# Two more slots, a smaller DMA scratch and one wide last group of y in a fused attention and feed-forward kernel

## The chip, the cores and the metric

The kernel runs on one core of one Trainium2 chip. The metric is the device time of one execution in microseconds (us), smaller is better; a single profiled execution supplies the trace. TensorE is called PE in the rows, VectorE DVE, ScalarE ACT, GpSimd POOL, SyncE SP.

## What is computed

Attention with rotary positions over 2 batches, 8 heads, 576 positions and 64 values per head, then two feed-forward blocks on the 1152 x 512 result x:

```python
a = x @ w_a                  # 512 -> 1536
b = x @ w_b
x = (a * b) @ w_out          # the first block; its result is called y in the kernel
h = x @ w_in                 # 512 -> 2048
g = h - np.tanh(h)
out = g @ w_out2             # the second block
```

The weights of both blocks arrive as 64-bit floats, seen by the kernel as pairs of 32-bit integers.

## The kernel before

**Precision.** Every matmul of the feed-forward blocks is done in three: each operand is split into a high part (a copy that rounds) and a low part (what is left), and high x high, high x low and low x high are added in PSUM (`mm3`, L517; the o matmuls do the same at L1204).

**Weights.** A list `units` (L407) fixes the order in which weights are brought in: for the first block ("ab", f) for each of its 12 chunks of 128, with ("o", f // 2) for each pair; for the second block ("i", n) and ("2", n), n = 0 to 7, in the order i0, i1, 2_0, 2_1, i2, i3, 2_2, 2_3 and so on. ("i", n) holds w_in for chunks 2n and 2n + 1, ("2", n) holds w_out2 for the same two chunks. Each unit is one DMA (two for "ab") on SyncE's queue into one of two staging tiles `st` (L428), and then a conversion in four pieces (`conv_unit`, L448): ScalarE scales one word and VectorE shifts the other (L457, L458); VectorE combines them in two passes (L460, L464), and after the second ScalarE casts the high part into its final place (L481); VectorE subtracts for the low part (L483). The staging tile is free for the next DMA when L483 is done. `cv(n)` emits n pieces and is called between the matmul groups; `get_w` (L500) emits whatever is missing where a matmul asks for it.

The final place of an "ab" or "i" weight is one of two halves of a tile `w0`, if one is free at that moment in the order of the code. Otherwise, and always for "o" and "2", it is a tile of the common pool `slots`, of which weights may hold `wcap` at a time: 6 (WC1) in the first block, 4 (WC2) in the second. `retire` (L505) gives the place back in that order once the last matmuls that read the weight are emitted.

**The common pool.** `slots` (L1045) has 12 tiles of 9 KB per partition. They hold `tmpa` for the whole rest of the kernel, the weights just named, the products `g` of the chunks (high and low part of a * b in the first block, of h - tanh(h) in the second), and in the second block `tmpb` and, for its chunks 0 and 1 only, `hs`. A tile that finds no free slot waits until one is released.

**First block.** For each chunk f, `ab_unit` (L1059) does 3 x 24 matmuls for a and b (three stretches of 384 tokens), ScalarE copies a out of PSUM (L1064), VectorE multiplies by b (L1065), ScalarE casts the high part of g (L1068) and VectorE subtracts for the low part (L1069). After every second chunk, 12 y units are queued, one for each of 3 stretches of tokens and 4 stretches of 128 outputs; six are emitted after each of the next chunks. A y unit (`y_unit`, L1075) is 6 matmuls, over the two chunks of its group, into one PSUM bank, and then a sum into `yacc`: a ScalarE copy for the first group (L1086), a VectorE addition for the other five (L1088). In the last group each unit also splits its sum for the second block: ScalarE casts `yh` (L1096), and the subtraction for `yl` (L1097) is on VectorE for odd d and on GpSimd for even d. The last group's units use only the four PSUM banks of one side, since the four of the other side go to the second block.

**Second block.** For each of its 16 chunks, `h_unit` (L1142) does 36 matmuls into one of two PSUM tiles of three banks, taken in turn. Then follows a chain between ScalarE and VectorE: squares (L1164, L1167), a mask written into g's tile (L1168), a polynomial (L1169, L1174), tanh (L1173), h - tanh (L1177), the choice between the two (L1178), the high part (L1179) and the low part (L1180). L1168 is the first write into a new g, so it is what waits for a slot. Chunk f + 2 can use chunk f's PSUM tile when L1177 is done; chunks 0 and 1 are first copied to `hs` (L1159), so that tanh is the last reader. After every four chunks, 9 o units (`o_unit`, L1188) are queued, each 12 matmuls of 512 columns over the group's four chunks for 128 tokens, and three are emitted after each of the next chunks. The sum into `oacc` is a ScalarE copy for the first group (L1210) and a VectorE addition later (L1212); the o units of all groups but the last share two PSUM banks. The last group's results leave by DMA.

**Order.** Up to the end of the attention a list written by hand orders all engines. From there on the framework's scheduler orders each engine's instructions: what is emitted first goes first among what is ready by the scheduler's own estimate, so a matmul group can be started in parts. On the chip each engine then works in that fixed order.

Of the kernel before, what the change touches and what calls it, by code (L numbers as in the profile page):

```python
CFG = {'WC1': 6, 'WC2': 4, 'CY': 1, 'CA': 2, 'CH': 2, 'OE': 3, 'PA': 99, 'PB': 0, 'PO': 4, 'GA': 0, 'GB': 0, 'WF': 99, 'WCE': 5, 'NH': 2, 'HA': 0, 'NT2': 2, 'NW': 20, 'TM': 1, 'CO': 1, 'CHB': 0, 'WG': 99, 'WCG': 4, 'XL': 7}
# [1 line left out]

# [13 lines left out]
ALU = mybir.AluOpType  # L17
# [341 lines left out]
def attention_moe_kernel(  # L359
# [13 lines left out]
    nc = tc.nc  # L373
# [4 lines left out]
    P = 128  # L378
    NPAIR = H // 2
    KC = DM // P  # L380
    NF1 = FF1 // P
# [4 lines left out]
    NP3 = 3  # L386
    TP = NT // NP3
    NTT = NT // P
    CW = 9
    globals().update(CFG)  # L390

    def hp(k):
        o = CFG.get('P_' + k, 0)
        return tc.high_priority(offset=o) if o else nullcontext()
# [100 lines left out]
    def cv(n):  # L495
        for _ in range(n):
            if not next(pieces, False):
                break

    def get_w(key):  # L500
        while key not in conv:
            assert next(pieces)
        return conv[key][0]

    def retire(key):  # L505
        hold = conv.pop(key)[1]
        if hold is None:
            nslot[0] -= 1
        else:
            wfree.append(hold)  # L510
# [6 lines left out]
    def mm3(ps, w, x, start, stop):  # L517
        for n, (a, c) in enumerate(((0, 0), (0, 1), (1, 0))):
            nc.tensor.matmul(ps, w(a), x(c), start=start and n == 0, stop=stop and n == 2)  # L519
# [3 lines left out]
    def m_tile(name, side=None):  # L523
        nps[0] += 1
        return psm[nps[0] % len(psm) if side is None else side].tile([P, 512], F32, tag="m", name=name)[:, 0:TP]
# [3 lines left out]
    def ab_mm(f, t):  # L529
        if (f, t) in ab_ps:  # L530
            return
        wc = get_w(("ab", f)).rearrange("p s (m c f) -> p s m c f", m=2, c=KC)
        r = []
        for m in range(2):
            ps = m_tile("ab")
            for c in range(KC):
                mm3(
                    ps, lambda s: wc[:, s, m, c],
                    lambda s: xt[s][:, c, t * TP:(t + 1) * TP], c == 0, c == KC - 1,
                )  # L540
            r.append(ps)
        ab_ps[f, t] = r


    with ExitStack() as actx:
# [48 lines left out]
        ps = {}  # L594
# [33 lines left out]
        def half(j):  # L628
            return slice(64 * j, 64 * j + 64)
# [385 lines left out]
        for i in range(2):  # L1015
            nc.vector.tensor_copy(
                out=qb[half(i), :, half(1 - i)], in_=zero[half(i)].rearrange("p (s x) -> p s x", s=2)
# [24 lines left out]
                conv["ab", f] = (cbuf["w0"][:, f], f)  # L1042


    slots = ctx.enter_context(tc.tile_pool(name="slots", bufs=12))  # L1045
    cbuf["slots"] = slots
    wcap[0] = WC1
    tmpa = slots.tile([P, 2, NP3, TP], F32, tag="slot", name="tmpa")
# [4 lines left out]
    with m2ctx:  # L1053
        psm.append(m2ctx.enter_context(
            tc.tile_pool(name="ps_m2", bufs=4, space=bass.MemoryType.PSUM, side="left")
        ))
        pf = {}

        def ab_unit(f):  # L1059
            a = tmpa[:, f % 2]  # L1060
            for t in range(NP3):
                ab_mm(f, t)
                r = ab_ps.pop((f, t))
                nc.scalar.copy(out=a[:, t], in_=r[0])  # L1064
                nc.vector.tensor_tensor(out=a[:, t], in0=a[:, t], in1=r[1], op=ALU.mult)  # L1065
                cv(1)
            g = slots.tile([P, 2, NP3, TP], F32R, tag="slot", name="g")
            nc.scalar.copy(out=g[:, 0], in_=a)  # L1068
            (nc.gpsimd if GA <= f < GB else nc.vector).tensor_tensor(out=g[:, 1], in0=a, in1=g[:, 0], op=ALU.subtract)  # L1069
            pf[f] = g  # L1070
            retire(("ab", f))

        GY = 2

        def y_unit(g, t, d):  # L1075
            last = g == NF1 // GY - 1
            ps = m_tile("y", 1 if last else None)
            for c in range(GY):
                wc = get_w(("o", (g * GY + c) // 2)).rearrange("p s (c d) -> p s c d", c=2)
                mm3(  # L1080
                    ps, lambda s: wc[:, s, c % 2, d * P:(d + 1) * P],
                    lambda s: pf[g * GY + c][:, s, t], c == 0, c == GY - 1,
                )
            o = yacc[:, d, t * TP:(t + 1) * TP]
            if g == 0:
                nc.scalar.copy(out=o, in_=ps)  # L1086
            else:
                nc.vector.tensor_tensor(out=o, in0=o, in1=ps, op=ALU.add)  # L1088
            if (t, d) == (NP3 - 1, KC - 1):
                for c in range(0, GY, 2):  # L1090
                    retire(("o", (g * GY + c) // 2))
            if last:
                if not yt:
                    yt.extend(actp.tile([P, KC, NT], F32R, tag="act", name=f"yt{s}") for s in range(2))
                yh, yl = (z[:, d, t * TP:(t + 1) * TP] for z in yt)
                nc.scalar.copy(out=yh, in_=o)  # L1096
                (nc.vector if d % 2 else nc.gpsimd).tensor_tensor(out=yl, in0=o, in1=yh, op=ALU.subtract)  # L1097

        yq = []
        for f in range(NF1):  # L1100
            if f == WF:
                wcap[0] = WCE
            ab_unit(f)
            for n in range(6):
                if yq:
                    y_unit(*yq.pop(0))
                if n < 4:
                    cv(CA)
            if f % GY == GY - 1:
                yq += [(f // GY, t, d) for t in range(NP3) for d in range(KC)]  # L1110
        while yq:
            y_unit(*yq.pop(0))
            cv(CY)
        mctx.close()
        ps_h = [ctx.enter_context(
            tc.tile_pool(name="ps_hr", bufs=1, space=bass.MemoryType.PSUM, side="right")
        )]
        ps_o = [ctx.enter_context(
            tc.tile_pool(name="ps_or", bufs=1, space=bass.MemoryType.PSUM, side="right")
        )]  # L1120
# [160 lines left out]
```

## Time and profile before

| | us |
|---|---|
| median of 3 executions (lowest to highest) | 596.63 (595.89 to 598.09) |
| the profiled execution, its own time | 598.46 |
| its span from the first to the last instruction | 596.6 |
| TensorE busy in the span | 578.5 |
| VectorE, ScalarE, GpSimd busy | 470.2, 348.5, 129.9 |

The profiled execution's own time is its span and 1.9 us around it. A busy time says how long an engine had an instruction under way; matmuls overlap in the pipeline, so for TensorE the count of matmuls and their start times tell more than its busy share. "[idle before <-X]" behind a row is how long the engine had stood idle and which instruction's end released it. The granted clock is the share of 2.4 GHz that TensorE was given.

### The profile page before, as it was taken

The page shows a single profiled execution, that of the slowest core. Times are in us where ns is not written, and L with a number is a line of the kernel's source. Part 1 is how long each engine was busy: PE and PEld are TensorE (multiplying, and loading weights), DVE is VectorE, ACT ScalarE, POOL GpSimd, SP SyncE. Part 2 cuts the span into 40 slices and gives each one's busy share as a digit, 9 for nine tenths or more (in the row PEclk, how much of TensorE's full clock was granted, in tenths as well). Part 3 has the DMA queues.
Part 4 walks back from the last instruction along what each step waited for, and adds up shares of the span by engine and source line. Part 5 has one row for each costly group of instructions (what it writes and reads, how often), then busy time and mean ns, then how long its engine had stood idle before and what let it go on. Part 6 is the DMA issues. An engine that isn't in the chain of part 4 may idle for free.

```text
span 596.6 us, 9137 instructions
## 1 busy us (share of the span) xinstructions
PE 578.5 (97%) x3467; PEld 550.2 (92%) x3467; DVE 470.2 (79%) x621; ACT 348.5 (58%) x590; POOL 129.9 (22%) x144
## 2 busy tenths in 40 slices
PE   8999998999999999999999999989998999999997
PEld 7899998999999999999999999889886988988865
DVE  8889998899688786887674685989945799796572
ACT  3899998999644653343333233589645763654450
POOL 5999998444600000000000000400000000000000
PEclk9999999999999999999999999999998999999999
DMA  4687688663234444342330232211010401100024
GB/s 123 153 201 189 163 202 173 191 160 104 78 125 157 142 167 139 118 142 70 90 122 1 71 142 80 93 40 71 2 70 1 139 4 70 71 1 0 1 51 108
DMA packets 40763, 60.06 MB, mean 101 GB/s; under 512 B 6928, under 2 KB 25616, under 8 KB 40720
## 3 DMA queue, kind: packets, MB, share of 16 engines
q1 hardware_dynamic: 40256, 59.00, 34.2%
q8 instruction: 27, 0.44, 0.3%
q10 hardware_dynamic: 464, 0.49, 0.3%
q14 instruction: 16, 0.13, 0.1%
HBM read 43.06 MB, written 2.36 MB: 76 GB/s over the span
## 4 chain that ended last, share of the span: by engine, by line
PE 79%; DVE 7%; DMA 5%; ACT 5%; issue 2%; POOL 1%; SPq 1%; ACTq 0%; POOLq 0%; DVEq 0%
PE ab L519 25%; PE h L519 13%; PE o L1204 12%; PE y L519 9%; PE acc L832 5%; PE pss L775 5%; PE pst L796 4%; PE ow L1204 3%; DMA vr<-in_v_dram 1%; DMA qb<-thq 1%; ACT p L784 1%; DMA st<-in_moe_w_in_dram 1%; DMA st<-in_moe_w_out_dram 1%; POOL early L644 1%; DMA early<-in_k_dram 1%
## 5 line engine op out<-in xcount | busy, mean ns | idle before, releaser
L1204 PE MATMUL o<-wc,g 128*128 128x512 f32 x348 | 83.9, 392 | 2.3 <-ACT oacc L1210 2.3
L1204 PEld LDWEIGHTS o<-wc,g 128*128 128x128 f32 x348 | 64.7, 188 | 15.7 <-ACT oacc L1210 3.0
L519 PE MATMUL y<-g,wc 128*128 128x384 f32 x432 | 77.0, 335 | 1.0 <-DVE yacc L1088 1.0
L519 PEld LDWEIGHTS y<-g,wc 128*128 128x128 f32 x432 | 74.9, 188 | 1.6 <-DVE yacc L1088 1.6
L519 PE MATMUL ab<-xt,w 128*128 128x384 f32 x432 | 76.3, 335 | 0.0
L519 PE MATMUL ab<-xt,wc 128*128 128x384 f32 x432 | 75.8, 334 | 0.0
L519 PEld LDWEIGHTS ab<-xt,wc 128*128 128x128 f32 x432 | 75.0, 188 | 0.0
L519 PEld LDWEIGHTS ab<-xt,w 128*128 128x128 f32 x432 | 74.9, 188 | 0.0
L519 PE MATMUL h<-yt,w 128*128 128x384 f32 x360 | 66.2, 336 | 2.5 <-ACT tmpa L1173 1.6
L519 PEld LDWEIGHTS h<-yt,w 128*128 128x128 f32 x360 | 62.6, 188 | 5.4 <-ACT tmpa L1173 1.9
L780 DVE TENSOR_REDUCE nm<-pss 128x1 f32<-128x576 f32 x72 | 53.9, 750 | 8.8 <-PE pss L775 8.0
L457 ACT ACTIVATE st<-st 128x1024 f32<-128x1024 f32 x30 | 35.2, 1175 | 42.9 <-DMA st<-in_moe_w_b_dram 21.2
L832 PE MATMUL acc<-ph,v 128*128 128x288 f32 x300 | 55.9, 309 | 0.0
L1097 POOL TENSOR_TENSOR yt<-yacc,yt 128x384 fp32r<-128x384 f32 x6 | 7.8, 1297 | 218.0 <-ACT yt L1096 218.0
L784 ACT ACTIVATE p<-pss,nm 128x576 f32<-128x576 f32 x72 | 54.2, 753 | 1.6 <-DVE nm L780 1.4
L803 DVE TENSOR_TENSOR ph<-pst,ph 128x512 fp32r<-128x512 f32 x72 | 48.1, 683 | 1.9 <-ACT ph L799 1.6
L775 PE MATMUL pss<-k,q 128*128 128x288 f32 x224 | 41.5, 309 | 2.2 <-DMA vr<-in_v_dram 1.4
L832 PEld LDWEIGHTS acc<-ph,v 128*128 128x128 f32 x300 | 43.0, 189 | 0.2
L1064 ACT COPY tmpa<-ab 128x384 f32<-128x384 f32 x36 | 17.1, 479 | 44.7 <-PE ab L519 43.8
L799 ACT CAST ph<-pst 128x512 fp32r<-128x512 f32 x72 | 41.4, 592 | 3.0 <-PE pst L796 2.9
L460 DVE SCALAR_TENSOR_TENSOR st<-st 128x1024 int32<-128x1024 int32 x30 | 36.7, 1223 | 7.0 <-ACT st L457 6.5
L796 PE MATMUL pst<-ident,p 128*128 128x128 f32 x288 | 41.3, 273 | 0.0
(149 smaller groups left out, 1013.9 us busy)
## 6 DMA issues: line engine op xcount, KB each, us to landing
st<-in_moe_w_out_dram SPq DMA_DIRECT2D x14, 1024.0 KB, 4.8
st<-in_moe_w_in_dram SPq DMA_DIRECT2D x8, 1024.0 KB, 5.1
q<-thq SPq DMA_DIRECT2D x28, 256.0 KB, 3.8
st<-in_moe_w_a_dram SPq DMA_DIRECT2D x10, 512.0 KB, 3.7
st<-in_moe_w_b_dram SPq DMA_DIRECT2D x10, 512.0 KB, 4.7
k<-thk SPq DMA_DIRECT2D x28, 144.0 KB, 3.2
vr<-in_v_dram SPq DMA_DIRECT2D x16, 128.0 KB, 3.1
out_dram<-oacc SPq DMA_DIRECT2D x16, 128.0 KB, 2.3
```

The source lines that it names most:

```text
L457: nc.scalar.activation(out=xs.bitcast(F32), in_=xs.bitcast(F32), func=AF.Copy, scale=2.0 ** -112)
L460: (pe if PO & 1 else nc.vector).scalar_tensor_tensor(out=w, in0=xs, scalar=3, in1=w, op0=ALU.logical_shift_left, op1=ALU.bitwise_or)
L519: nc.tensor.matmul(ps, w(a), x(c), start=start and n == 0, stop=stop and n == 2)
L775: nc.tensor.matmul(s_ph(g)[:, a], st, mv[:, a * HS:(a + 1) * HS], start=(m == 0), stop=(m == len(mms) - 1))
L780: nc.vector.tensor_reduce(out=nm[i % 2][:, u:u + 1], in_=s_ph(g), axis=AX.XY, op=ALU.max, negate=True)
L784: nc.scalar.activation(out=po.rearrange("p (a x) -> p a x", a=2), in_=s_ph(g), func=AF.Exp, bias=nm[i % 2][:, u:u + 1], scale=1.0, accum_o ...
L796: nc.tensor.transpose(tile_of(g)[:, t * P:(t + 1) * P], pt[i % 2][:, t, o:o + P], ident)
L799: nc.scalar.copy(out=pslot(i, u)[:, 0, qm(i)], in_=tile_of(g))
L803: nc.vector.tensor_tensor(out=dst[:, 1, qm(i)], in0=tile_of(g), in1=dst[:, 0, qm(i)], op=ALU.subtract)
L832: nc.tensor.matmul(tile_of(g), st, pslot(i, u)[:, s, a * HS:(a + 1) * HS], start=first and s == 0, stop=last and s == 1,)
L1064: nc.scalar.copy(out=a[:, t], in_=r[0])
L1204: nc.tensor.matmul(ps, g[:, a, i * P:(i + 1) * P], wc[:, c, f % 2], start=(n == 0 and m == 0), stop=(n == GE - 1 and m == 2),)
```

## The change

The compiler's scratch for dynamic DMAs is set to 1 KB, the pool `slots` gets 14 tiles instead of 12, and weights may hold 7 of them in the first block (WC1) instead of 6. The groups of y are written out: chunks 0-1, 2-3, 4-5, 6-7 and then 8 to 11 as one group, whose 12 units are 12 matmuls long and are queued after chunk 11; between chunks 8 to 11 only the units of the group of chunks 6-7 are emitted, six after chunk 8 and six after chunk 9. So yacc is added to four times instead of five after the first copy. The subtractions for `yl` are all on VectorE. `YN`, 6 as before, only names a number.

```diff
-CFG = {'WC1': 6, 'WC2': 4, 'CY': 1, 'CA': 2, 'CH': 2, 'OE': 3, 'PA': 99, 'PB': 0, 'PO': 4, 'GA': 0, 'GB': 0, 'WF': 99, 'WCE': 5, 'NH': 2, 'HA': 0, 'NT2': 2, 'NW': 20, 'TM': 1, 'CO': 1, 'CHB': 0, 'WG': 99, 'WCG': 4, 'XL': 7}
+CFG = {'YN': 6, 'WC1': 7, 'WC2': 4, 'CY': 1, 'CA': 2, 'CH': 2, 'OE': 3, 'PA': 99, 'PB': 0, 'PO': 4, 'GA': 0, 'GB': 0, 'WF': 99, 'WCE': 5, 'NH': 2, 'HA': 0, 'NT2': 2, 'NW': 20, 'TM': 1, 'CO': 1, 'CHB': 0, 'WG': 99, 'WCG': 4, 'XL': 7}
...
-    slots = ctx.enter_context(tc.tile_pool(name="slots", bufs=12))
+    slots = ctx.enter_context(tc.tile_pool(name="slots", bufs=14))
...
-        GY = 2
+        GROUPS = [range(f, f + 2) for f in range(0, NF1 - 4, 2)] + [range(NF1 - 4, NF1)]
 
         def y_unit(g, t, d):
-            last = g == NF1 // GY - 1
+            last = g == GROUPS[-1]
             ps = m_tile("y", 1 if last else None)
-            for c in range(GY):
-                wc = get_w(("o", (g * GY + c) // 2)).rearrange("p s (c d) -> p s c d", c=2)
+            for f in g:
+                wc = get_w(("o", f // 2)).rearrange("p s (c d) -> p s c d", c=2)
                 mm3(
-                    ps, lambda s: wc[:, s, c % 2, d * P:(d + 1) * P],
-                    lambda s: pf[g * GY + c][:, s, t], c == 0, c == GY - 1,
+                    ps, lambda s: wc[:, s, f % 2, d * P:(d + 1) * P],
+                    lambda s: pf[f][:, s, t], f == g[0], f == g[-1],
                 )
...
                 nc.scalar.copy(out=yh, in_=o)
-                (nc.vector if d % 2 else nc.gpsimd).tensor_tensor(out=yl, in0=o, in1=yh, op=ALU.subtract)
+                nc.vector.tensor_tensor(out=yl, in0=o, in1=yh, op=ALU.subtract)
...
-            if f % GY == GY - 1:
-                yq += [(f // GY, t, d) for t in range(NP3) for d in range(KC)]
+            yq += [(g, t, d) for g in GROUPS if g[-1] == f for t in range(NP3) for d in range(KC)]
...
-    nc = _bacc.Bacc("TRN2", target_bir_lowering=False, num_devices=1)
+    nc = _bacc.Bacc("TRN2", target_bir_lowering=False, num_devices=1, dynamic_dma_scratch_size=1024)
```

## Rows read from the trace of the kernel before

**Rows 1.** The page's first part: busy time of the engines.

```profile
PE 578.5 (97%) x3467; PEld 550.2 (92%) x3467; DVE 470.2 (79%) x621; ACT 348.5 (58%) x590; POOL 129.9 (22%) x144
```

**Rows 2.** TensorE in order of time, 325 to 425 us: start, duration, engine, line.

```profile
350.17 12.64 PE L519 MATMUL ab<-xt,wc 128*128 128x384 f32 x72
362.65 14.73 PE L519 MATMUL y<-g,wc 128*128 128x384 f32 x84
378.10 1.32 PE L519 MATMUL y<-g,wc 128*128 128x384 f32 x6 [0.72 <-DVE yacc L1088]
379.69 3.39 PE L519 MATMUL y<-g,wc 128*128 128x384 f32 x18 [0.28 <-DVE yacc L1088]
382.93 12.64 PE L519 MATMUL h<-yt,wc 128*128 128x384 f32 x72
397.16 6.54 PE L519 MATMUL h<-yt,w 128*128 128x384 f32 x36 [1.59 <-ACT tmpa L1173]
```

**Rows 3.** The same, 421 to 500 us.

```profile
431.05 8.36 PE L1204 MATMUL o<-wc,g 128*128 128x512 f32 x36
439.25 6.43 PE L519 MATMUL h<-yt,wc 128*128 128x384 f32 x36
445.52 9.04 PE L1204 MATMUL o<-wc,g 128*128 128x512 f32 x39
456.84 0.96 PE L1204 MATMUL o<-wc,g 128*128 128x512 f32 x3 [2.28 <-ACT oacc L1210]
458.10 8.05 PE L519 MATMUL h<-yt,wc 128*128 128x384 f32 x36 [0.29 <-DVE tmpb L1177]
```

**Rows 4.** Busy time by stretch: length, then PE, PEld, DVE, ACT, POOL; clock, DMA.

```profile
363.00:383.00 20.00, 18.99 (x108) 18.35 (x108) 18.08 (x27) 10.93 (x15) 5.78 (x5) 1.00 0.31 106
...
439.25:484.69 45.44, 42.05 (x209) 38.21 (x208) 29.89 (x25) 26.82 (x27) 0.00 (x0) 0.96 0.14 47
484.69:559.47 74.78, 74.69 (x370) 66.56 (x369) 60.20 (x57) 38.16 (x35) 0.00 (x0) 1.00 0.08 29
559.47:593.60 34.13, 32.51 (x145) 25.89 (x143) 20.92 (x30) 10.17 (x18) 0.00 (x0) 1.00 0.26 57
```

**Rows 5.** The chain of waits, 383 to 397 us: start, duration, what.

```profile
383.67 1.14 DVE wc L483
...
384.87 5.03 DMA st<-in_moe_w_in_dram
...
389.98 1.19 ACT st L457
...
395.98 1.14 ACT tmpa L1173
```

**Rows 6.** One microsecond of the table by stretch; the granted clock is behind POOL.

```profile
460.00:461.00 1.00, 1.00 (x5) 1.00 (x4) 1.00 (x2) 0.32 (x1) 0.00 (x0) 0.50 0.00 0
```

**Rows 7.** All engines in order of time: ScalarE and VectorE on chunk 5.

```profile
434.62 1.27 ACT L1167 ACTIVATE tmpb<-tmpb,cst 128x1152 f32<-128x1152 f32 x1
...
451.88 1.26 ACT L1168 ACTIVATE g<-tmpb,cst 128x1152 fp32r<-128x1152 f32 x1
...
456.60 1.35 DVE L1177 TENSOR_TENSOR tmpb<-h,tmpb 128x1152 f32<-128x1152 f32 x1
```

**Rows 8.** The same for ScalarE on chunk 14.

```profile
557.63 1.26 ACT L1168 ACTIVATE g<-tmpa,cst 128x1152 fp32r<-128x1152 f32 x1 [3.73 <-PE o L1204]
```

**Rows 9.** VectorE's groups by line, 325 to 597 us: busy us, mean ns.

```profile
L1088 DVE TENSOR_TENSOR yacc<-yacc,y 128x384 f32<-128x384 f32 x30 | 15.3, 546 | 0.9 <-PE y L519 0.8
...
L460 DVE SCALAR_TENSOR_TENSOR st<-st 128x1024 int32<-128x1024 int32 x12 | 14.7, 1221 | 1.8 <-ACT st L457 1.6
...
L458 DVE TENSOR_SCALAR st<-st 128x1024 int32<-128x1024 int32 x12 | 8.7, 725 | 6.3 <-DMA st<-in_moe_w_in_dram 3.9 <-DMA st<-in_moe_w_out_dram 2.4
L1097 DVE TENSOR_TENSOR yt<-yacc,yt 128x384 fp32r<-128x384 f32 x6 | 5.4, 893 | 0.3 <-ACT yt L1096 0.3
```

**Rows 10.** All engines in order of time: the low part of g of chunk 11.

```profile
365.07 1.36 DVE L1069 TENSOR_TENSOR g<-tmpa,g 128x1152 fp32r<-128x1152 f32 x1 [0.63 <-ACT g L1068]
```

**Rows 11.** The page's groups of instructions: GpSimd after the attention.

```profile
L1097 POOL TENSOR_TENSOR yt<-yacc,yt 128x384 fp32r<-128x384 f32 x6 | 7.8, 1297 | 218.0 <-ACT yt L1096 218.0
```

More of the change, by code (lines that the diff above doesn't have):

```diff
@@ L1071, in ab_unit @@
             retire(("ab", f))
-        GY = 2
+        GROUPS = [range(f, f + 2) for f in range(0, NF1 - 4, 2)] + [range(NF1 - 4, NF1)]
         def y_unit(g, t, d):
-            last = g == NF1 // GY - 1
+            last = g == GROUPS[-1]
             ps = m_tile("y", 1 if last else None)
-            for c in range(GY):
-                wc = get_w(("o", (g * GY + c) // 2)).rearrange("p s (c d) -> p s c d", c=2)
-                mm3(
-                    ps, lambda s: wc[:, s, c % 2, d * P:(d + 1) * P],
-                    lambda s: pf[g * GY + c][:, s, t], c == 0, c == GY - 1,
+            for f in g:
+                wc = get_w(("o", f // 2)).rearrange("p s (c d) -> p s c d", c=2)
+                mm3(
+                    ps, lambda s: wc[:, s, f % 2, d * P:(d + 1) * P],
+                    lambda s: pf[f][:, s, t], f == g[0], f == g[-1],
                 )
             o = yacc[:, d, t * TP:(t + 1) * TP]
-            if g == 0:
+            if g[0] == 0:
                 nc.scalar.copy(out=o, in_=ps)
@@ L1089, in y_unit @@
             if (t, d) == (NP3 - 1, KC - 1):
-                for c in range(0, GY, 2):
-                    retire(("o", (g * GY + c) // 2))
+                for f in g[::2]:
+                    retire(("o", f // 2))
             if last:
@@ L1103, in attention_moe_kernel @@
             ab_unit(f)
-            for n in range(6):
+            for n in range(YN):
                 if yq:
```

## The prediction

> **What bounds the kernel now.** I read the busy shares first, then a table by stretch, then TensorE's own order of time, and last, for each hole in it, what ended the hole. TensorE (PE) is busy for 578.5 of 596.6 us [rows 1], so only its holes can be won back; a fuller VectorE costs nothing until TensorE waits for it. A dense stream of matmuls is the yardstick: 72 of 384 columns from 350.17 to 362.65 is 0.1733 us each, 36 of 512 columns from 431.05 to 439.25 is 0.2278 us each [rows 2, 3]. Against it the first product shows no hole up to 362.65, and the places that the change can reach lose this:
>
> - The last y sums: 84 + 6 + 18 = 108 matmuls should take 18.72 us and take 382.93 - 362.65 = 20.28 us, **1.56 us** lost, with VectorE named as releaser; VectorE is busy for 18.08 of the 20 us there [rows 2, 4].
> - Behind h chunks 0 and 1: 72 matmuls from 382.93 end at 395.41, the next start at 397.16, **1.75 us** [rows 2]. The chain of waits says why: VectorE finishes a weight conversion (L483) at 384.81, its staging tile is refilled by a DMA that lands at 389.90, ScalarE's next instruction (L457) is the one that reads it, and chunk 0's chain stands behind that up to the tanh that lets go of its PSUM tile [rows 5].
> - From 439.25 to 484.69 TensorE is idle for 45.44 - 42.05 = 3.39 us, and h chunk 7 takes 8.05 us where chunk 6 took 6.43, because the granted clock is 0.50 (1.2 GHz) right after the hole: **5.0 us** together [rows 3, 4, 6]. The hole comes from ScalarE: it finished L1167 of chunk 5 by 435.89 and wrote chunk 5's g (L1168) only at 451.88; TensorE then waits for ScalarE's copy (2.28 us) and for L1177 of that same chunk [rows 3, 7].
> - From 484.69 to 559.47 only 0.09 us is idle; in the last stretch 36 x 0.1733 + 108 x 0.2278 = 30.84 us of matmuls and a last sum of about 0.7 us fill 34.13 us, **2.6 us** lost [rows 4]. There too a write of g (chunk 14) waited, 3.73 us, for TensorE's o matmuls, and its lateness pushes chunk 15 back [rows 8].
>
> **The change part by part.** Times of the sum are taken off the profiled execution, 598.46 us (span 596.6 and 1.86 around it); it lies 1.83 above the median of 596.63, and I put the same difference on the median.
>
> *Slots, 12 to 14.* Counted through the code: when chunk 5's g is asked for, the pool holds tmpa, tmpb, the four w_out weights of the second product, ("i", 3), whose chunks 6 and 7 are not done, and g0 to g4: 12 of 12. So L1168 has to wait until the o matmuls of group 0 let g0 go. With WC1 = 7 one more first-stage weight is converted early, so ("i", 2) and ("i", 3) land in the two w0 halves and ("i", 1) in the pool, where it is gone after chunk 3. Then the pool holds 2 + 4 + g0 to g7 = 14 of 14, and chunks 5, 6 and 7 wait for no slot. Chunk 5's L1168 goes to about 436, its L1177 some 4 us later (L1168 to the end of L1177 is 451.88 to 457.95 in the row, with chunk 6's work between) [rows 7], long before TensorE wants chunk 7 at 445.52 + 36 x 0.2278 = 453.7 [rows 3]. Late next is chunk 7's own chain, with h chunk 8 and the two o banks as cover. Bounds 0 and -5.0; I take **-4.5**, near the full hole, since the next group of chunks, with six g's free, lost 0.09 us.
>
> *The same slots at the end.* Of g8 to g15 none waits: 2 + 4 + 8 = 14. Chunk 14's write of g comes up to 3.7 us sooner. Bounds 0 and -2.6; chunk 15's own chain is still in the open, so **-1.6**.
>
> *Four chunks in one group.* 12 sums L1088 of 0.546 us leave VectorE (6.6 us) [rows 9]; they lay beside dense matmuls, so this alone gives nothing. What counts is the drain: a last unit is 12 matmuls = 2.08 us and not 1.04, for one sum, one cast and one subtraction, so 1.1 us of VectorE per 2.08 us of TensorE. The holes before 378.10 and 379.69 go: -1.56. New is a wait for chunk 11: its low part ends at 366.43, 3.8 us after its last matmul [rows 10], and six y units no longer lie between. Cover: four PSUM banks' worth of chunks 8 to 10, 4 x 9 x 0.1733 = 6.2 us, if they are ordered so; if not, 3.8 - 1.56 = 2.2 us. I take +0.4, near the covered end, because o units of the next group are already started in such parts (39 = 36 + 3 at 445.52) [rows 3]. Net **-1.2**, bounds -1.56 and +0.6.
>
> *Low parts on VectorE.* Six GpSimd subtractions leave (1297 ns each) [rows 11], six go to VectorE. There the six that it has take 893 ns in the mean, where L1088 of the same size takes 546; 6 x 0.35 = 2.1 us is time beside GpSimd [rows 9]. Twelve of 0.546 make 6.6 us against 5.4, +1.2 us, covered by the doubled pace above. If that cover is gone, it is 1.2 us. The Trainium skill (SBUF — State Buffer, Summary: rules for kernel authors) says that VectorE and GpSimd instructions block each other in full when the VectorE one reads two SBUF inputs and the GpSimd one reads SBUF, whichever issues second. By it up to 7.8 us of GpSimd work could have stood before VectorE; the trace bears out about 2.1, and since the drain lost 1.56 in all, by the rule the sum would gain 0.4 more at most.
>
> *The conversion before h.* With VectorE less full, L483 of the last w_out weight, and with it the DMA that ended at 389.90, comes earlier; it also has a free slot in the pool at once. The 1.75 us behind chunk 1 goes or stays whole; I take **-1.5**, since VectorE's lateness heads that chain [rows 5].
>
> *Late weights.* The price of the new places: ("i", 4) must wait for the w0 half of ("i", 2), free after chunk 5 and not after chunk 3, and everything behind comes about one unit later. One conversion is 0.73 + 3 x 1.22 = 4.39 us of VectorE [rows 9]; it moves into stretches where VectorE is busy for 60.20 of 74.78 us [rows 4]. Bounds 0 and +4.4; **+1.0**, near the lower end, since there is room.
>
> *Scratch.* The page's list of DMA issues names SyncE and ScalarE alone and GpSimd never, so a scratch of 1 KB costs 0; it only makes the room.
>
> Sum: -4.5 - 1.6 - 1.2 - 1.5 + 1.0 = **-7.8 us**, so 590.7 for an execution like the profiled one and **588.8** at the median.
>
> **The rivals.** *The wait moves.* Chunk 5 gets its slot but h chunk 8 then waits for ("i", 4), or the o banks hold TensorE; for it speaks that the w0 half is free two chunks later, against it that chunks 6 and 7 and the rest of group 0's o matmuls lie in between. Then only -1.2 - 1.5 is left: 593.9. *Late weights decide (slower).* In the order of the code ("i", 6) is now converted in the turn of chunk 11 and needed by chunk 12, ("i", 7) just ahead of chunk 14. Exposed whole, with refill 5.03, L457 1.19, two combining passes 2.44, a cast (taken as L457, 1.19) and L483 1.14 [rows 5, 9], that is 11.0 us; two o banks of nine matmuls cover 4.1. Twice 6.9 and twice the slow restart of 1.6 is 17.0, against gains of 8.8: 604.8. It decides only if L483 of ("i", 6) ends after chunk 11's h matmuls and the cover; its w0 half is free from chunk 7 on, so the early steps can run ahead, which speaks against. *The parts don't do what they say.* The extra slots go unused because the order is fixed as before, and y was dense anyway: 596.6. *All holes close*: -1.56 - 1.75 - 5.0 - 2.6 and a little of what the idle times don't count: about 584.6.
>
> **How the numbers follow.** The forecast 0.66 (its own range 585 to 592.5), the moved wait 0.15, late weights 0.08, nothing 0.05, all holes 0.06. A measurement here can tell about 0.5%, 3 us, from no change: 593.6 and 599.6 are the borders. The forecast, all holes and a fifth of the moved wait make faster 0.75; the rest of it and nothing 0.17; late weights 0.08. The range 584.5 to 595.5 leaves out late weights, nothing and a few per cent of each tail.
>
> **What would show it.** Right: g's L1168 with no TensorE releaser, h chunk 7 starting right behind the o matmuls of group 0 in 6.4 us at a granted clock of 1.00, y units of 12 matmuls without a hole, 48 sums L1088 on VectorE, no GpSimd work after attention. Wrong: a hole ahead of chunks 8, 12 or 14 released by L483, or one at the first y unit released by L1069.

## The result: 588.69 us, and the profile after

The changed kernel takes **588.69 us** (median of 4 runs, 587.81 to 589.61) against 597.36 us for the kernel before on the same chip (4 runs, 595.89 to 598.60): ratio **0.9856, 95% interval 0.9826 to 0.9886**. The profiled execution took 589.61 us with a span of 587.8 us, 8.8 us less than the span before.

The first part of its page answers to [rows 1]: TensorE's busy time falls by 2.2 us and the span by 8.8, so most of what went is idle time.

```profile
PE 576.3 (98%) x3467; PEld 549.8 (94%) x3467; DVE 465.7 (79%) x615; ACT 349.7 (59%) x590; POOL 122.1 (21%) x138
```

TensorE in order of time, after (start, duration, engine, line; the lines behind L1097 are one lower than before):

```profile
356.91 25.45 PE L519 MATMUL y<-g,wc 128*128 128x384 f32 x144
382.20 18.05 PE L519 MATMUL h<-yt,wc 128*128 128x384 f32 x102
...
428.71 8.36 PE L1203 MATMUL o<-wc,g 128*128 128x512 f32 x36
436.91 6.43 PE L519 MATMUL h<-yt,w 128*128 128x384 f32 x36
443.18 8.36 PE L1203 MATMUL o<-wc,g 128*128 128x512 f32 x36
451.38 12.67 PE L519 MATMUL h<-yt,w 128*128 128x384 f32 x72
```

The y matmuls stand as one block of 144 with no bracket of idle time in it, where [rows 2] show two. The third chunk of h follows without the hole of 1.59 us. The last o matmuls of group 0 come in 36 and 36, and h chunk 7 begins straight behind them; before they came in 36 and 39, and 3 more behind the hole (by the count of matmuls the last 3 of the 39 and those 3 already belong to group 1) [rows 3]. ScalarE, after, shows why (L1166 and L1167 of chunk 5, then L1167 of chunk 6):

```profile
430.93 1.26 ACT L1166 ACTIVATE tmpb<-tmpb,cst 128x1152 f32<-128x1152 f32 x1
432.10 1.24 ACT L1167 ACTIVATE g<-tmpb,cst 128x1152 fp32r<-128x1152 f32 x1
...
445.71 1.24 ACT L1167 ACTIVATE g<-tmpa,cst 128x1152 fp32r<-128x1152 f32 x1
```

The write of g follows straight on the step ahead of it in the same chunk's chain, in chunk 6 too (L1166 at 444.55). Before, the write of chunk 5 stood at 451.88, 16 us behind that step [rows 7], and it has no bracket of its own: in ScalarE's order it came behind chunk 6's squares and four copies of group 0's sums, and the bracket is on the last of these copies:

```profile
451.20 0.59 ACT L1210 COPY oacc<-o 128x512 f32<-128x512 f32 x1 [2.13 <-PE o L1204]
```

So the missing tile has to be read from the order of ScalarE's instructions, from what stands between the two steps of one chunk; the idle time of the write alone doesn't show it. The busy time by stretch answers to [rows 4] (length, then PE, PEld, DVE, ACT, POOL; clock, DMA):

```profile
356.91:382.20 25.29, 25.29 (x145) 24.93 (x145) 20.25 (x31) 10.77 (x16) 0.00 (x0) 1.00 0.25 84
436.91:501.43 64.52, 64.47 (x325) 58.34 (x324) 54.72 (x50) 39.19 (x38) 0.00 (x0) 1.00 0.19 66
501.43:551.51 50.08, 50.08 (x254) 45.27 (x252) 41.67 (x40) 27.37 (x24) 0.00 (x0) 1.00 0.06 21
551.51:584.80 33.29, 31.89 (x145) 26.00 (x143) 17.52 (x28) 8.70 (x16) 0.00 (x0) 1.00 0.27 59
```

The list of TensorE's waits from 325 us on has one entry left:

```profile
PE ow L1203 <- DVE oacc L1211: 0.6, 1, 0.6
```

**One table for all kernels.** The first matmul of the first product (ab) starts at 160.78 us before and at 161.28 after, and somewhere from 159.29 to 162.02 in the thirteen profiles of this study, although no edit of a kernel here is to a line of that stage. So I read the profiles from that start on, in three stretches of TensorE's order of time: to the start of h chunk 6 (436.91 after, 439.25 before), from there to the start of h chunk 15 (551.51, 559.47), and from there to the end of the span.

| kernel | to h6 | h6 to h15 | h15 to end | sum |
|---|---|---|---|---|
| before | 278.47 | 120.22 | 37.13 | 435.82 |
| after | 275.63 | 114.60 | 36.29 | 426.52 |
| e1: before + 14 tiles | 278.56 | 115.28 | 36.27 | 430.11 |
| e9: before + 13 tiles | 278.37 | 114.77 | 36.30 | 429.44 |
| e2: before + WC1 = 7 | 278.25 | 117.68 | 36.83 | 432.76 |
| e10: before + WC1 = 5 | 280.22 | 115.01 | 36.90 | 432.13 |
| e12: before + wide group | 276.18 | 114.89 | 36.91 | 427.98 |
| e3: e12 + low parts on VectorE | 275.96 | 114.89 | 36.85 | 427.70 |
| e4: e3 + WC1 = 7 (after, 12 tiles) | 276.28 | 114.70 | 36.21 | 427.19 |
| e11: e3 with 11 tiles | 277.25 | 128.09 | 40.61 | 445.95 |
| e8: before + low parts on VectorE | 277.41 | 119.83 | 36.92 | 434.16 |
| e5: after, low parts in turn again | 275.66 | 114.80 | 36.23 | 426.69 |
| e6: after, groups of two again | 277.47 | 115.06 | 36.27 | 428.80 |

By this table the change gains 2.84 us ahead of chunk 6, 5.62 between chunks 6 and 15, and 0.84 at the end: 9.30, of which the later start of the first product (0.50) hides a part.

### The profile page after: what moved, and what is told of

Read it like the earlier page. It is cut to its first block, busy times and chain, and to the rows that moved or that the text cites. A ratio compares the mean times of both kernels' runs of the same rounds, so it can differ in the third digit from the quotient of the medians.

```text
span 587.8 us, 9112 instructions
## 1 busy us (share of the span) xinstructions
PE 576.3 (98%) x3467; PEld 549.8 (94%) x3467; DVE 465.7 (79%) x615; ACT 349.7 (59%) x590; POOL 122.1 (21%) x138
## 4 chain that ended last, share of the span: by engine, by line
PE 83%; DMA 5%; ACT 4%; DVE 3%; SPq 2%; issue 1%; POOL 1%; ACTq 0%; DVEq 0%; POOLq 0%
PE ab L519 25%; PE h L519 14%; PE y L519 13%; PE o L1203 11%; PE pss L775 5%; PE acc L832 5%; PE pst L796 4%; PE ow L1203 3%; DMA st<-in_moe_w_out_dram 1%; SPq L724 1%; DMA early<-in_k_dram 1%; POOL early L644 1%; PE psp L699 1%; DMA k<-thk 1%; DMA q<-thq 1%
## 5 line engine op out<-in xcount | busy, mean ns | idle before, releaser
L1203 PEld LDWEIGHTS o<-wc,g 128*128 128x128 f32 x348 | 64.7, 188 | 13.6 <-ACT g L1178 0.8
L460 DVE SCALAR_TENSOR_TENSOR st<-st 128x1024 int32<-128x1024 int32 x30 | 36.6, 1224 | 5.5 <-ACT st L457 5.0
L519 PE MATMUL h<-yt,wc 128*128 128x384 f32 x216 | 38.4, 336 | 0.0
```

The source lines that it names most:

```text
L460: (pe if PO & 1 else nc.vector).scalar_tensor_tensor(out=w, in0=xs, scalar=3, in1=w, op0=ALU.logical_shift_left, op1=ALU.bitwise_or)
L1203: nc.tensor.matmul(ps, g[:, a, i * P:(i + 1) * P], wc[:, c, f % 2], start=(n == 0 and m == 0), stop=(n == GE - 1 and m == 2),)
```

## The experiments

Times are compared with runs of the kernel before taken with them: 597.36 us for e1 to e4, 597.45 for e8 to e11, 599.05 for e5, e6 and e12.

**e1: the tiles alone.** The kernel before with

```diff
-    slots = ctx.enter_context(tc.tile_pool(name="slots", bufs=12))
+    slots = ctx.enter_context(tc.tile_pool(name="slots", bufs=14))
-    nc = _bacc.Bacc("TRN2", target_bir_lowering=False, num_devices=1)
+    nc = _bacc.Bacc("TRN2", target_bir_lowering=False, num_devices=1, dynamic_dma_scratch_size=1024)
```

> The kernel before with one part of the change alone: 14 slots (and the 1 KB scratch that makes room). Theory of the slots (chunk 5's g waits for a slot): 14 hold tmpa, tmpb, five weights and g0 to g6, so chunks 5 and 6 no longer wait; the hole ahead of h chunk 7 closes and chunk 14's g waits no longer: 5.6 + 0.8 us gained, ratio about 0.989, while the y drain (1.56 us) and the 1.75 us behind h chunk 1 stay. Rival (the weights' places decide, so slots alone do little): under 2 us gained, ratio above 0.996, chunk 5's L1168 still released late.

Measured: 592.22 us (591.26 to 593.09), ratio 0.9911 [0.9876, 0.9945]. TensorE in order of time, e1:

```profile
376.58 1.33 PE L519 MATMUL y<-g,wc 128*128 128x384 f32 x6 [0.70 <-DVE yacc L1088]
...
395.76 4.43 PE L519 MATMUL h<-yt,w 128*128 128x384 f32 x24 [1.69 <-ACT tmpa L1173]
...
444.12 8.36 PE L1204 MATMUL o<-wc,g 128*128 128x512 f32 x36
452.32 6.43 PE L519 MATMUL h<-yt,wc 128*128 128x384 f32 x36
```

The two losses in front (y, chunk 1) stay as in [rows 2] and the hole ahead of h chunk 7 is gone. So a wait for a tile made that hole, and tiles close it.

**e2: the seventh early weight alone**, in 12 tiles: the kernel before with `'WC1': 7`.

> The kernel before with WC1 = 7 alone, still 12 slots. Theory of the slots with the weights' places: (i, 3) lies in w0, so 12 slots hold two temporaries, four weights and g0 to g5; chunk 5 does not wait, chunk 6 waits for g0 as chunk 5 did, but h chunk 8 comes late enough to cover it: about 5 us gained, ratio near 0.9915, while the end (chunk 14) stays as before. Rival (only the pool's size counts): no gain, ratio 1.000, or a loss of up to 4.4 us from weights converted one unit later.

Measured: 596.05 us (594.89 to 597.10), ratio 0.9976 [0.9957, 0.9996]. The step of the prediction that has WC1 = 7 clear a tile falls. TensorE, e2:

```profile
457.38 0.96 PE L1204 MATMUL o<-wc,g 128*128 128x512 f32 x3 [2.28 <-ACT oacc L1210]
458.64 6.51 PE L519 MATMUL h<-yt,w 128*128 128x384 f32 x36 [0.29 <-DVE tmpb L1177]
464.99 5.19 PE L519 MATMUL h<-yt,wc 128*128 128x384 f32 x29
```

The hole is [rows 3] over again. The input names tell where the weights lie: `w` is a w0 half, `wc` a tile of the pool. Chunk 7 now reads `w`, so ("i", 3) did move to a half, as the prediction said; but chunk 8 reads `wc`, and in the kernel before it is chunks 6 and 7 that do [rows 3]. The tile that ("i", 3) left was taken by ("i", 4). Counted again through the code with this in mind: 2 + 5 weights + g0 to g4 = 12, as before. The trace agrees that one more weight is converted: VectorE has run L483 25 times when chunk 0's chain begins, 24 times in the kernel before.

**e4: the whole change in 12 tiles**, the kernel after with

```diff
-    slots = ctx.enter_context(tc.tile_pool(name="slots", bufs=14))
+    slots = ctx.enter_context(tc.tile_pool(name="slots", bufs=12))
```

> The changed kernel with 12 slots instead of 14, all else as changed. Theory of the slots with the weights' places: chunk 5 has its slot with 12 too, so only the end's 0.8 us is lost against the changed kernel: about 7.5 us gained on the kernel before, ratio near 0.987. Rival (the two extra slots carry the gain): the hole near h chunk 7 or 8 is back with about 5 us, only 3 us are gained, ratio near 0.995.

Measured: 588.75 us (587.98 to 591.22), ratio 0.9860 [0.9826, 0.9895]: within the noise the change keeps its whole gain without its two tiles. The profile shows a small part that they do pay for, 0.65 us ahead of chunk 6, where the wait behind chunk 1 is back in part:

```profile
393.98 6.52 PE L519 MATMUL h<-yt,wc 128*128 128x384 f32 x36 [0.83 <-ACT tmpa L1172]
```

**e3: the same with WC1 = 6**, so the wide group and the low parts, and of pool and weights only the scratch of 1 KB: the kernel after with 12 tiles and `'WC1': 6`.

> The changed kernel with 12 slots and WC1 = 6, so the y part alone (the wide last group, low parts on VectorE). Theory: the y drain gains 1.2 us, the wait behind h chunk 1 goes with it (1.5 us): 2.7 us gained, ratio near 0.9955, with the hole ahead of h chunk 7 as before. Rival (y was dense, the wait behind chunk 1 belongs to the weights' places): at most 0.5 us gained in all, ratio 0.999 to 1.003.

Measured: 589.57 us (588.69 to 591.12), ratio 0.9867 [0.9835, 0.9899], about three times the gain that I had expected: the hole ahead of chunk 7 is closed here too. ScalarE, e3, chunks 5 and 6:

```profile
432.49 1.26 ACT L1167 ACTIVATE g<-tmpb,cst 128x1152 fp32r<-128x1152 f32 x1
...
448.59 1.26 ACT L1167 ACTIVATE g<-tmpa,cst 128x1152 fp32r<-128x1152 f32 x1
```

Chunk 5 finds a tile; chunk 6, 16.1 us behind it (13.6 in the kernel after), waits for g0, and h chunk 7 covers that. Why is there a tile? Read through the code, the wide group gives back ("o", 4) and ("o", 5) together with its last unit, where groups of two give ("o", 4) back at the end of their fifth group. Under the same cap one weight fewer has then been converted when h begins (L483 has run 23 times when chunk 0's chain begins, here and in e12, 24 times in the kernel before), and the cap of the second product (WC2 = 4) keeps it so: 2 + 4 weights + g0 to g4 = 11 of 12 when chunk 5 asks. Three edits of the number of weights and tiles were made to test this count.

The scratch was not tried apart. It doesn't decide the hole: e10 closes it without the small scratch, and e11 has it with one. The DMA issues that the traces list, before and after, are on SyncE and ScalarE alone (the page shows only the largest, all on SyncE).

**e9: one tile more**, the kernel before with `bufs=13` (and the scratch at 1 KB).

> The kernel before with 13 tiles in the pool instead of 12 (and the scratch at 1 KB for room). Theory A, the count of tiles: when h chunk 5 asks for its g, the pool holds 2 temporaries, 5 converted weights and g0 to g4, 12 in all; a thirteenth tile is enough for chunk 5, and only chunk 6 then waits, with h chunk 7 and the o matmuls as cover. The hole ahead of h chunk 7 goes, as it did with 14: about 592 us, ratio 0.991, L1168 of chunk 5 near 435 us without a TensorE releaser, L1168 of chunk 6 with one. Rival B, both tiles are needed: chunk 6 waits and TensorE stands later by about the same: 595 to 597 us, ratio 0.997 to 1.000. The drain of y (1.56 us lost) and the wait behind chunk 1 (1.75) stay under both.

Measured: 592.56 us (591.17 to 592.87), ratio 0.9912 [0.9895, 0.9928]: theory A. ScalarE, e9:

```profile
435.66 1.26 ACT L1168 ACTIVATE g<-tmpb,cst 128x1152 fp32r<-128x1152 f32 x1
...
451.76 1.26 ACT L1168 ACTIVATE g<-tmpa,cst 128x1152 fp32r<-128x1152 f32 x1
```

One tile does what two do. Chunk 6's write still comes 16.1 us behind chunk 5's, after the copies of group 0, but TensorE has no hole for it.

**e10: one weight fewer**, the kernel before with `'WC1': 5`, against the direction of the change.

> The kernel before with one number edited against the direction of the change: WC1 = 5 instead of 6 (the change has 7), 12 tiles in the pool, groups of two. Theory A, the count: in the order of the code one weight fewer is then held, w_out2 pair 3 is converted only behind chunk 7's turn, and at chunk 5 the pool holds 2 + 4 + g0 to g4 = 11 of 12; chunk 5 gets its tile and the hole ahead of h chunk 7 goes: about 592 us, ratio 0.991. Rival B, fewer weights converted early make the weights late: the first unit of group 1's o sums that needs pair 3, or h chunk 8, waits for L483, 2 to 5 us more than A: 594 to 599 us, ratio 0.995 to 1.003, with L483 as releaser in the trace. Rival C, the hole is not a matter of the number of tiles but of the wide last group: 597 us, ratio 1.000, hole as before.

Measured: 594.24 us (592.79 to 595.00), ratio 0.9943 [0.9927, 0.9960]. The count holds: from h6 to h15 it takes 115.01 us, as with more tiles, and rival C falls. But it loses 1.75 us ahead of chunk 6. TensorE, e10:

```profile
396.02 6.51 PE L519 MATMUL h<-yt,wc 128*128 128x384 f32 x36 [1.13 <-ACT tmpa L1173]
...
404.78 6.54 PE L519 MATMUL h<-yt,wc 128*128 128x384 f32 x36 [0.74 <-ACT tmpb L1173]
...
413.95 6.50 PE L519 MATMUL h<-yt,w 128*128 128x384 f32 x36 [0.62 <-DVE tmpa L1177]
```

The chain of waits of e10 shows steps of a weight conversion (L458, L460) on VectorE in the middle of a chunk's own chain:

```profile
403.01 1.27 DVE tmpb L1174
404.28 0.60 DVE st L458
404.88 1.27 DVE tmpb L1177
...
408.79 1.22 DVE st L460
410.01 1.26 DVE tmpa L1174
```

So B's price is real, 1.75 us, though by another releaser than the L483 that I had named.

**e11: eleven tiles under the wide group**, e3 with `bufs=11`.

> The kernel after with WC1 = 6 and 11 tiles instead of 14 (12 tiles and WC1 = 6 gave 589.6 us). Theory A, the count: with the wide last group the pool holds 2 + 4 + g0 to g4 = 11 at chunk 5, so with 11 tiles chunk 5 waits again for the o matmuls of group 0, and the hole of 3.3 us ahead of h chunk 7 (and perhaps the slow restart of 1.6 us) comes back: 593 to 594.5 us, ratio 0.992 to 0.995, L1168 of chunk 5 near 450 us with TensorE as releaser. Rival B, the wide group closes the hole by its timing and not by a free tile: 589.6 us, ratio 0.987, no hole.

Measured: 608.20 us (607.36 to 611.04), ratio 1.0184 [1.0162, 1.0206]. A's direction, at four to five times its price: 18.6 us more than e3, where 3.4 to 4.9 were expected. TensorE, e11:

```profile
455.69 0.96 PE L1203 MATMUL o<-wc,g 128*128 128x512 f32 x3 [2.28 <-ACT oacc L1209]
456.95 7.92 PE L519 MATMUL h<-yt,wc 128*128 128x384 f32 x36 [0.29 <-DVE tmpb L1176]
...
534.72 1.28 PE L519 MATMUL h<-yt,wc 128*128 128x384 f32 x4 [2.16 <-DVE tmpa L1176]
...
566.19 7.89 PE L519 MATMUL h<-yt,wc 128*128 128x384 f32 x36 [2.48 <-DVE tmpb L1176]
...
580.78 1.16 PE L1203 MATMUL ow<-wc,g 128*128 128x512 f32 x3 [1.81 <-ACT g L1178]
```

The hole is back at chunk 7 to the hundredth of [rows 3]. What I had not counted is that later chunks run short of tiles as well: three more holes of 2.16, 2.48 and 1.81 us, with the matmuls behind two of them slowed (4 h matmuls in 1.28 us, 36 in 7.89).

**e8: the low parts alone**, the kernel before with

```diff
-                (nc.vector if d % 2 else nc.gpsimd).tensor_tensor(out=yl, in0=o, in1=yh, op=ALU.subtract)
+                nc.vector.tensor_tensor(out=yl, in0=o, in1=yh, op=ALU.subtract)
```

> The kernel before with one edit: all twelve low parts of y on VectorE instead of every second one on GpSimd. Theory A, pace: VectorE gets six more instructions of about 0.55 us and loses about 2 us of slow ones beside GpSimd, net +1.2 us in a drain that already waits for it; the drain of y loses 1.56 + 1.2 = 2.8 us, 598.5 us, ratio 1.002. Rival B, the two engines block each other: without GpSimd VectorE's mean L1097 falls from 893 to about 550 ns and each of the six hand-overs to GpSimd goes; the drain loses under 1 us and the time is 596.5 us, ratio 0.998. The times differ by less than a measurement can tell, so the trace of the drain decides: TensorE's time from the first y unit behind chunk 11 to h chunk 0 (20.28 us in the kernel before) is 21.5 under A, 19.5 under B. The hole ahead of h chunk 7 stays under both.

Measured: 596.20 us (595.04 to 599.85), ratio 0.9984 [0.9967, 1.0000]; the trace decides. TensorE, e8:

```profile
362.61 15.88 PE L519 MATMUL y<-g,wc 128*128 128x384 f32 x90
378.33 1.20 PE L519 MATMUL h<-yt,wc 128*128 128x384 f32 x6
379.37 3.31 PE L519 MATMUL y<-g,wc 128*128 128x384 f32 x18
382.52 11.60 PE L519 MATMUL h<-yt,wc 128*128 128x384 f32 x66
394.65 6.51 PE L519 MATMUL h<-yt,w 128*128 128x384 f32 x36 [0.53 <-ACT tmpa L1173]
...
411.50 6.48 PE L519 MATMUL h<-yt,w 128*128 128x384 f32 x36 [0.62 <-DVE tmpa L1177]
```

VectorE's groups in e8, 325 to 590 us (busy us, mean ns):

```profile
L1097 DVE TENSOR_TENSOR yt<-yacc,yt 128x384 fp32r<-128x384 f32 x12 | 6.3, 550 | 0.1
```

Rival B holds. Twelve low parts on VectorE take 6.3 us where six beside GpSimd took 5.4 [rows 9]. The drain from 362.61 to 382.52 holds 114 matmuls, 114 x 0.1733 = 19.76 us, and lasts 19.91: dense, where [rows 2] lost 1.56. A share of that comes back as a hole ahead of chunk 4 (the last row), and 1.06 us is left by h chunk 6. VectorE's subtraction reads two SBUF tiles and so does GpSimd's. The Trainium skill (SBUF — State Buffer, Summary: rules for kernel authors) says that such a pair block each other; 893 ns in company against 550 ns alone agrees with it.

**e5: the low parts in turn again, under the wide group.** The edit of e8 undone in the kernel after.

> The kernel after with one edit undone: every second low part of y goes back to GpSimd. Theory A, pace: with units of 12 matmuls VectorE has 2.08 us per unit and the slower instructions beside GpSimd are covered; 589.0 us, ratio 0.986, y of 144 matmuls still 25.3 us to h chunk 0. Rival B, GpSimd still holds the drain up as it did with groups of two (there its removal gave 0.8 us back in the drain and 1.0 behind chunk 1): y takes 25.7 to 26.1 us, the wait behind chunk 1 is 1 us again, 590 to 590.7 us, ratio 0.988 to 0.989.

Measured: 589.98 us (588.48 to 590.55), ratio 0.9851 [0.9831, 0.9871]. Theory A. TensorE, e5:

```profile
357.64 25.40 PE L519 MATMUL y<-g,wc 128*128 128x384 f32 x144
382.88 19.07 PE L519 MATMUL h<-yt,wc 128*128 128x384 f32 x108
```

VectorE's low parts are slower again (six of 690 ns in the mean), and nobody waits: y takes 25.24 us, as after. Moving the low parts is worth 1 us with groups of two and nothing with the wide one.

**e6: groups of two again**, in the kernel after.

```diff
-        GROUPS = [range(f, f + 2) for f in range(0, NF1 - 4, 2)] + [range(NF1 - 4, NF1)]
+        GROUPS = [range(f, f + 2) for f in range(0, NF1, 2)]
```

> The kernel after with one edit undone: six y groups of two chunks, with 14 tiles, WC1 = 7 and the low parts on VectorE kept. Theory A, the count: at chunk 5 the pool holds 2 + 5 + g0 to g4 = 12 of 14, so the hole ahead of h chunk 7 stays closed although WC1 = 7 alone, with 12 tiles, left it open; what comes back is about 0.9 us of the drain and up to 0.5 behind chunk 1 as with the low parts alone on VectorE: 590 to 591 us, ratio 0.988 to 0.990. Rival B, with WC1 = 7 and groups of two the six weights held make chunk 6 or 7 wait and the hole moves there: 593 to 595 us, ratio 0.993 to 0.997.

Measured: 591.61 us (590.07 to 592.29), ratio 0.9886 [0.9868, 0.9904]: theory A. The stretch to chunk 6 is that of e8 (277.47 and 277.41), the two behind it are near those of e1 (115.06 and 36.27 here, 115.28 and 36.27 there). So with groups of two the other edits add up to most of the change.

**e12: the wide group alone**: the kernel before with its last four chunks in one y group; 12 tiles, WC1 = 6, low parts in turn. It keeps the change's scratch of 1 KB.

```diff
-        GY = 2
+        GROUPS = [range(f, f + 2) for f in range(0, NF1 - 4, 2)] + [range(NF1 - 4, NF1)]
```

> The kernel before with the wide last y group alone: 12 tiles, WC1 = 6, low parts on VectorE and GpSimd in turn. Theory A, the count and the doubled pace: at chunk 5 the pool holds 2 + 4 + g0 to g4 = 11 of 12, so the hole is closed without a tile more, and the drain is dense to about 0.5 us: 589.5 to 590.5 us, ratio 0.987 to 0.989. Rival B, the low parts are needed as well: the drain and the wait behind chunk 1 stay as they were, hole closed: 592 us, ratio 0.991. Rival C, without more tiles or VectorE's low parts nothing is gained: 597 us, ratio 1.000.

Measured: 590.15 us (589.64 to 591.80), ratio **0.9862** [0.9843, 0.9882]. Theory A. TensorE, e12:

```profile
357.78 25.49 PE L519 MATMUL y<-g,wc 128*128 128x384 f32 x144
383.11 12.64 PE L519 MATMUL h<-yt,wc 128*128 128x384 f32 x72
395.96 6.54 PE L519 MATMUL h<-yt,w 128*128 128x384 f32 x36 [0.20 <-ACT tmpa L1172]
...
444.47 8.36 PE L1203 MATMUL o<-wc,g 128*128 128x512 f32 x36
452.67 6.43 PE L519 MATMUL h<-yt,wc 128*128 128x384 f32 x36
```

All three holes of the middle are closed or down to 0.20 us by this one part; in the table it leaves 427.98 - 426.52 = 1.46 us to the rest of the change, less than the two intervals can tell apart. No kernel of the study was measurably faster than the kernel after.

## Why the prediction was right, and which step of it was not

The time (588.8 forecast, 588.69 measured) and the range held. That they meet to 0.1 us is luck: 7.8 us off 596.63 was forecast and 8.67 off 597.36 was measured, so a higher start and a larger gain nearly cancel. By its own steps:

- **The bounds.** TensorE's holes were all there was to win, and of the three in the middle none is left: confirmed.
- **Slots, -4.5.** Measured with the middle as a whole, 120.22 - 114.60 = **5.62 us**, 0.6 over the bound. The hole ahead of chunk 7 was a missing tile: e1 and e9 close it with tiles, e10 with one weight fewer, and e11 opens it again. What failed is the working "With WC1 = 7 one more first-stage weight is converted early, so ("i", 2) and ("i", 3) land in the two w0 halves": true, but the tile that comes free is refilled (e2: 117.68 us in that stretch, hole unchanged). And two tiles were not needed for this hole: one is enough (e9), and none under the wide group (e4, e12). I had put the group's effect on the pool at nothing, while it holds one weight back and so pays this term by itself.
- **The end, -1.6.** Mis-sized: 37.13 - 36.29 = **0.84 us**. I had taken chunk 14's wait for a tile as its cause. In e4 that write still waits 3.7 us for the o matmuls, and the end is as short as after (36.21); in e3 and e12 it waits as well and the end is 36.85 and 36.91. What goes with a short end is how soon ScalarE begins chunk 15's chain: 6.46 or 6.47 us behind the start of h chunk 15, released by chunk 15's own matmuls, in every profile whose end is 36.2 or 36.3, and 7.23 or 7.24 us, straight behind its last step for chunk 14, in every other but e11's. A tile gets there by an early write of chunk 14's g. WC1 = 7 under the wide group, the one edit from e3 to e4, gets there without: in e3, as before, a weight conversion (L483, 1.22 us) stands on VectorE in the middle of chunk 14's chain; in e4 the last L483 begins at 538.32, 12 us ahead of h chunk 15. Either way some 1.8 of the 2.6 us stay.
- **Four chunks in one group, -1.2.** 20.28 us of drain against 25.29 less six units that moved behind its start (6 x 6 x 0.1733 = 6.24) is 19.05: **-1.23**. The new wait for chunk 11 at the first unit did not come.
- **Low parts, in the y term.** The doubled pace covers them, as forecast: e5 is as fast without. With groups of two they are worth 1.06 us by chunk 6 (e8), where the sum priced them at up to 1.2 of loss; the trace of before gave a hint in the 893 ns, and it was the right one.
- **The conversion before h, -1.5.** From h chunk 0 to chunk 6: 439.25 - 382.93 = 56.32 before, 436.91 - 382.20 = 54.71 after, **-1.61**. The step held: the last L483 ahead of that chain ends at 363.52 and not at 384.81, ScalarE reads the refilled staging tile at 371.30 and not at 389.98, and its first instruction for chunk 0 (L1158, at 388.64) is released by h's own matmuls. VectorE's load isn't the whole reason: e12 has most of the gain alone, with one weight fewer to convert (438.20 - 383.11 = 55.09), e1 has none; in e4, with VectorE's work as after but without the tiles, that L483 ends at 381.50 and half of the hole stays.
- **Late weights, +1.0.** **0**: from the end of group 1's o matmuls to chunk 15 it is 559.47 - 509.41 = 50.06 before and 50.08 after. The price of weight work at a bad place exists (e10, 1.75 us), but in the first chunks of h and not where I had put it.
- **The rivals.** No wait moved to chunk 8, no late weight decided; "the parts don't do what they say" was half true of the pool, whose tiles chunk 5 uses but would not have needed.

Measured in the same order, -5.62 - 0.84 - 1.23 - 1.61 + 0 = -9.30, plus 0.50 of a later start, is -8.80 against the -7.8 of the sum. Two errors, a slots term short by 1.1 and a late-weights term that was not there, are partly offset by the end.

## What to carry to other kernels

When one pool feeds two consumers, count its tiles at the moment of the wait, and count again after every edit that changes when something is given back: here a regrouping of sums in the stage before freed a tile and closed the hole, while an edit that seemed to free one had it taken by the next in line. Run the parts alone before paying for all of them: one of the four parts had the whole measurable gain, and two others were each worth something only in its absence. The tile name in a matmul's row is enough to see where a weight was put.

## What the runs showed of the hardware

The same hole does not always bring the half clock. In the profiles of the kernel before, of e2, e8 and e11 TensorE stands 2.28 us at the same place for the same reason; the granted clock behind it is 0.50 (1.2 GHz) for some 3 us in the kernel before [rows 6], in e8 and in e11, and stays at 1.00 (2.4 GHz) in e2. The table by stretch, one microsecond of each, first e2:

```profile
460.00:461.00 1.00, 1.00 (x8) 1.00 (x6) 1.00 (x1) 0.00 (x0) 0.00 (x0) 1.00 0.00 0
```

and e11:

```profile
458.00:459.00 1.00, 1.00 (x4) 1.00 (x4) 1.00 (x2) 0.00 (x0) 0.00 (x0) 0.50 0.00 0
```

The 36 matmuls of chunk 7 take 6.51 us in e2 and 8.05 in the kernel before, so 1.5 of the 2.5 us that e2's profile gains between chunks 6 and 15 is this and not the count of tiles. It needs no edit: of the 41 executions of the kernel before that were taken with the experiments, 13 had a granted clock of 1.000 in the mean and a median of 596.67 us, the other 28 one of 0.991 to 0.997 and 598.30 us. What decides it no run here shows. And the start of the first product moves by 2.7 us (159.29 to 162.02) between the profiles, about as much as the smaller parts of this change are worth.
